# The first K load of a cached-attention decode kernel, issued as two halves with the half that is transposed first in front

## The chip, the cores and the metric

The kernel runs on one core of one Trainium2 chip. The metric is the device time of one execution in microseconds (us); lower is better. Every execution also has a span, from the first instruction to the last, which in these runs is 1.8 to 2.2 us shorter than the time.

## The reference, cut to what matters

One token attends to a cache of 65,536 positions with 8 key/value heads, two query heads to each. A small token MLP and a gate are mixed in at the end; they cost almost nothing (the page of the kernel before gives VectorE and ScalarE 0% each of the chain that ended last).

```python
# x: 1x1x448   k_cache, v_cache: 1 x 8 x 65536 x 256, bf16 (268 MB each)
q = (x @ wq).reshape(B, Sq, 16, 256).transpose(0, 2, 1, 3)
k = jnp.repeat(k_cache, 2, axis=1);  v = jnp.repeat(v_cache, 2, axis=1)
scores = jnp.einsum("bhqd,bhkd->bhqk", q, k) * (256 ** -0.5)
o = jnp.einsum("bhqk,bhkd->bhqd", softmax(scores), v)
a = o.transpose(0, 2, 1, 3).reshape(B, Sq, 4096) @ wo
return g * a + (1 - g) * b          # g: gate, b: token MLP
```

## The kernel before

The caches are streamed in 32 blocks of 8.39 MB for K and as many for V; I call them K0, V0, K1, V1 and so on. A block is 128 partitions of 128 rows (NV = 128), and HV = 64 is half of that. All large loads are issued by SyncE, in order, on one queue that spreads over 16 DMA engines (each load leaves 16 landing records in the trace, and by the page below q1 takes 99.5% of the time of 16 engines).

```python
for j in range(NP):                                   # SyncE, NP = 32
    last = j == NP - 1
    if j >= 1:
        eng.wait_ge(sem_tr[NB - 1], BODY * (j - 1) + DC)   # half of K(j-1) is transposed
    load(kring, A_k_cache, j, 0, HV if last else NV, HV * (j % 2), sem_k)
    if last:
        load(kring, A_k_cache, j, HV, NV, HV, sem_kb)
    if j == 0:
        eng.wait_ge(s_q, 1); eng.wait_ge(s_hb, 1)          # query projection is done
    else:
        eng.wait_ge(sem_pv, j)                             # values of block j-1 are done
    load(vbuf, A_v_cache, j, 0, NLATE if last else NV, 0, sem_v)
    # ... the pieces of the last V, and the output weights wo once per head
```

The K ring holds one and a half blocks. The V buffer holds one block. So V1 cannot be issued before the tensor engine (PE) has finished all the value matmuls of block 0, whatever the queue is doing.

On the PE a block is 8 chunks. Each chunk is transposed through PSUM, copied out by VectorE and ScalarE, and scored; then come the value matmuls of the whole block.

```python
def transposes(k, c, j, u16, x2):
    if k == 0:
        pe.wait_ge(sem_k, u16)            # u16 = 16 * (j + 1)
    if k == DC:                           # DC = 4
        with pe.If(j == NP - 1):
            pe.wait_ge(sem_kb, 16)
    # ... chunks 0 to 3 read rows 64 to 127 of an even block, chunks 4 to 7 rows 0 to 63

def values(j, c0, u16):
    # ... denominators, then 128 matmuls acc <- vbuf, pT
    some(0, NLATE).then_inc(s_early, 1)
    some(NLATE, NV).then_inc(sem_pv, 1)   # all but the last block
```

The softmax here doesn't subtract the row's maximum and nothing guards it: scores larger than these inputs give would overflow.

## Time and profile before

| | |
|---|---|
| time, median of 3 runs | 1267.47 us (1267.24 to 1267.68) |
| the profiled execution | 1268.64 us, span 1266.8 us |
| bytes read | 544.2 MB, 430 GB/s over the span |
| steady pace, from the landings | one block in 19.35 us, 433.5 GB/s |

These lines are from the page of the kernel before: the span, the bytes moved in 40 equal slices of it, and the queues with packets, MB and share of the 16 engines' time.

```profile
span 1266.8 us, 38663 instructions
...
GB/s 411 430 417 430 432 430 441 430 432 432 430 441 430 432 430 432 441 430 432 430 432 441 430 432 430 432 441 430 430 432 430 443 430 430 432 430 443 430 416 350
...
q1 hardware_dynamic: 12264, 544.22, 99.5%
q8 instruction: 8, 0.13, 0.0%
```

The q1 queue is the SyncE loads and fills the engines for 99.5% of the span: the kernel is bound by its loads.

The chain of waits of the kernel before, in its first 125 us, has the columns start, duration (both us) and what took it. "issue" is time in which the engine waited for nothing that the profile shows.

```profile
1.65 30.86 DMA kring<-in_A_k_cache_dram
...
32.64 6.43 PE kst L278 x32
...
49.55 0.85 issue
...
55.74 2.62 issue
...
60.99 2.01 PE acc L330 x28
63.00 2.77 issue
65.77 4.34 PE acc L330 x92
...
73.87 6.30 PE kst L278 x32
...
85.38 27.35 DMA kring<-in_A_k_cache_dram
```

The PE starts when K0 has landed, works through block 0 with stops of 0.85, 2.62 and 2.77 us that have no stated cause, and the chain follows the PE all the way into block 1 at 73.87 us.

The timeline of the SyncE queue (start us, duration us, engine, line, operation, tiles) shows when K1, V1, K2 and V2 were issued:

```profile
44.27 0.34 SPq L221 DMA_DIRECT2D kring<-in_A_k_cache_dram  x1
70.15 0.33 SPq L221 DMA_DIRECT2D vbuf<-in_A_v_cache_dram  x1
85.38 0.33 SPq L221 DMA_DIRECT2D kring<-in_A_k_cache_dram  x1
101.89 0.33 SPq L221 DMA_DIRECT2D vbuf<-in_A_v_cache_dram  x1
```

V1 goes out at 70.15 us. The stretches of one microsecond around it (start and end, length, busy time and instruction count of each engine, then PE clock, DMA share and GB/s) show the queue running dry:

```profile
69.00:70.00 1.00, 1.00 (x39) 0.68 (x31) 0.00 (x0) 0.00 (x0) 0.00 (x0) 1.00 0.91 393
70.00:71.00 1.00, 0.11 (x4) 0.00 (x0) 0.00 (x0) 0.00 (x0) 0.00 (x0) 1.00 0.07 16
71.00:72.00 1.00, 0.00 (x0) 0.00 (x0) 0.00 (x0) 0.00 (x0) 0.00 (x0) 1.00 2.17 786
72.00:73.00 1.00, 0.02 (x4) 0.03 (x4) 0.00 (x0) 0.00 (x0) 0.00 (x0) 0.70 0.67 262
```

A data packet is booked at its start and takes 2.42 us, so single microseconds swing widely. Read the 16 GB/s of 70 to 71 us together with the packets that were still in flight: counting those in the trace, the 16 engines lose 0.50 us each on average between 69.4 and 73 us, and under 0.05 us in all the rest from 5 to 1259 us.

### The profile page before, as it was taken

What the parts mean: (1) busy time and instruction counts of PE and PEld (TensorE: products, weight loads), DVE (VectorE), ACT (ScalarE), POOL (GpSimd) and SP (SyncE); (2) the same over time, 40 slices, a digit from 0 to 9 for tenths busy, and PEclk for the clock granted to TensorE, in tenths of its full rate; (3) what the DMA queues carried; (4) which work ended last, traced back from release to release, by engine and by line L of the source; (5) the groups of instructions that cost most, each with busy time, mean ns of one, the idle gap of its engine ahead of it and who ended that gap; (6) DMA issues with size and microseconds to landing.
All of it is one profiled execution on the core that took longest, in us unless ns stands there. A gap on an engine that the chain in (4) does not pass through costs nothing.

```text
span 1266.8 us, 38663 instructions
## 1 busy us (share of the span) xinstructions
PE 911.8 (72%) x17041; PEld 862.0 (68%) x17041; DVE 418.1 (33%) x741; ACT 537.4 (42%) x786; POOL 0.9 (0%) x7
## 2 busy tenths in 40 slices
PE   1886678766787666787666876768767688666698
PEld 1776668766677666686666876658766578665687
DVE  2433334333344233443222332223322233331233
ACT  0543345533355333454334553335533345432455
POOL 0000000000000000000000000000000000000000
PEclk9988789788898788888788888789887788887989
DMA  9999999999999999999999999999999999999998
GB/s 411 430 417 430 432 430 441 430 432 432 430 441 430 432 430 432 441 430 432 430 432 441 430 432 430 432 441 430 430 432 430 443 430 430 432 430 443 430 416 350
DMA packets 12365, 544.39 MB, mean 430 GB/s; under 512 B 1344, under 2 KB 3394, under 8 KB 3778
## 3 DMA queue, kind: packets, MB, share of 16 engines
q1 hardware_dynamic: 12264, 544.22, 99.5%
q8 instruction: 8, 0.13, 0.0%
q10 hardware_dynamic: 90, 0.01, 0.0%
q14 instruction: 3, 0.02, 0.0%
HBM read 544.22 MB, written 0.00 MB: 430 GB/s over the span
## 4 chain that ended last, share of the span: by engine, by line
DMA 68%; PE 30%; issue 1%; SPq 0%; DVE 0%; ACT 0%; ACTq 0%
DMA kring<-in_A_k_cache_dram 66%; PE kst L278 25%; PE sps L298 5%; DMA vbuf<-in_A_v_cache_dram 2%; PE acc L330 1%; PE sps L350 0%; SPq L221 0%; PE acc L322 0%; PE prj L370 0%; ACT pT L615 0%; SPq L218 0%; SPq L216 0%; DVE out_g L590 0%; PE prj L431 0%; DVE oTn L548 0%
## 5 line engine op out<-in xcount | busy, mean ns | idle before, releaser
L278 PE MATMUL kst<-ident,kring 128*128 128x128 f32 x4096 | 561.6, 298 | 310.5 <-DMA kring<-in_A_k_cache_dram 308.6
L626 ACT ACTIVATE ktT<-kst 128x1024 bf16<-128x1024 bf16 x512 | 499.6, 1021 | 668.1 <-PE kst L278 667.8
L278 PEld LDWEIGHTS kst<-ident,kring 128*128 128x128 f32 x4096 | 511.8, 155 | 320.2 <-issue 318.0
L532 DVE COPY ktT<-kst 128x1024 bf16<-128x1024 bf16 x512 | 354.3, 692 | 771.4 <-PE kst L278 748.1
L298 PEld LDWEIGHTS sps<-qcur,ktT 128*128 128x128 bf16 x8192 | 237.8, 96 | 6.5 <-issue 3.9
L298 PE MATMUL sps<-qcur,ktT 128*128 128x2 bf16 x8192 | 236.7, 163 | 3.5 <-issue 3.5
L330 PE MATMUL acc<-vbuf,pT 128*2 128x256 bf16 x4064 | 144.2, 310 | 3.5 <-issue 2.8
L330 PEld LDWEIGHTS acc<-vbuf,pT 128*2 128x2 bf16 x4064 | 107.4, 95 | 31.9 <-issue 3.3
L615 ACT ACTIVATE pT<-sps 128x32 f32 x256 | 51.8, 202 | 18.6 <-PE sps L298 18.6
L322 PE MATMUL acc<-pT,ones_sq 128*128 128x32 bf16 x256 | 11.7, 178 | 12.3 <-ACT pT L615 12.3
L322 PEld LDWEIGHTS acc<-pT,ones_sq 128*128 128x128 bf16 x256 | 8.6, 97 | 15.2 <-ACT pT L615 14.9
L632 ACT ACTIVATE z_b<-z_b 128x448 bf16<-128x448 bf16 x14 | 8.1, 577 | 20.5 <-DVE z_b L519 20.5
L537 DVE COPY accs<-acc 128x288 f32<-128x288 f32 x8 | 3.7, 458 | 39.6 <-PE acc L330 39.6
L394 PE MATMUL acc<-vbuf 42*128 42x42 bf16 x1 | 0.2, 216 | 8.6 <-DMA b_b<-in_B_b_dram 8.6
L523 DVE TENSOR_SCALAR z_b<-z_b 128x448 bf16<-128x448 bf16 x14 | 3.9, 277 | 6.8 <-ACT z_b L632 6.8
L394 PEld LDWEIGHTS acc<-vbuf 42*128 42x128 bf16 x1 | 0.1, 100 | 8.7 <-DMA b_b<-in_B_b_dram 8.7
L525 DVE TENSOR_TENSOR gu<-wtmp,z_b 128x448 bf16<-128x448 bf16 x14 | 5.5, 393 | 1.0
L517 DVE TENSOR_TENSOR z_b<-u_b,wtmp 128x448 bf16<-128x448 bf16 x14 | 5.5, 393 | 1.0
L513 DVE TENSOR_TENSOR z_b<-wtmp,u_b 128x448 bf16<-128x448 bf16 x14 | 5.5, 393 | 1.0
L511 DVE TENSOR_TENSOR wtmp<-u_b 128x448 bf16<-128x448 bf16 x14 | 5.5, 392 | 1.1
L507 DVE TENSOR_SCALAR wtmp<-hbT,params 128x448 bf16<-128x448 bf16 x14 | 4.7, 337 | 2.6 <-issue 2.6
L509 DVE TENSOR_SCALAR u_b<-wtmp,params 128x448 bf16<-128x448 bf16 x14 | 4.7, 336 | 2.6 <-issue 2.6
(84 smaller groups left out, 76.5 us busy)
## 6 DMA issues: line engine op xcount, KB each, us to landing
kring<-in_A_k_cache_dram SPq DMA_DIRECT2D x2, 4096.0 KB, 22.7
vbuf<-in_A_v_cache_dram SPq DMA_DIRECT2D x1, 6144.0 KB, 24.3
wo_sb<-in_A_wo_dram SPq DMA_DIRECT2D x8, 448.0 KB, 28.6
vbuf<-in_A_wq_dram SPq DMA_DIRECT2D x1, 3072.0 KB, 10.3
vbuf<-in_A_v_cache_dram SPq DMA_DIRECT2D x1, 1024.0 KB, 26.4
vbuf<-in_A_v_cache_dram SPq DMA_DIRECT2D x1, 768.0 KB, 27.4
vbuf<-in_A_wq_dram SPq DMA_DIRECT2D x1, 512.0 KB, 11.1
kring<-in_A_k_cache_dram SPq DMA_DIRECT2D x31, 27.9
```

The source lines that it names most:

```text
L278: ins = pe.transpose(kst[:, b, i * P:(i + 1) * P], kring_f[:, at + NT * (k % DC) + 4 * b + i, :], ident[:, :])
L298: ins = pe.matmul(sps[:, par, 2 * nt:2 * nt + 2], ktT[:, par, b, ntl * DH + dj:(ntl + 1) * DH:2], qcur[:, dj, :], start=(dj == 0), stop=(d ...
L322: pe.matmul(acc[:, DENC:SELC], ones_sq[:, :], pT[:, r, :], start=False, stop=(r == BODY - 1), skip_group_check=True)
L330: ins = pe.matmul(acc[o:o + REP, 0:DH], pT[:, r, 2 * nt:2 * nt + 2], vbuf[:, n, :], start=False, stop=False, skip_group_check=True)
L511: vec.tensor_tensor(W, U, U, op=ALU.mult)
L513: vec.tensor_tensor(Z, W, U, op=ALU.mult)
L517: vec.tensor_tensor(Z, U, W, op=ALU.add)
L525: vec.tensor_tensor(gu[:, :], W, Z, op=ALU.mult).then_inc(s_pb, 1)
L532: vec.tensor_copy(ktT[:, k % KTB, b, :], kst_b[:, b, :]).then_inc(sem_ev[b], 1)
L615: act.activation(pT[:, bass.ds(p0 + k % DC, 1), :].rearrange("p o n -> p (o n)"), sps[:, k % 2, 0:2 * NT], AF.Exp, scale=scale).then_inc(s ...
L626: act.activation(ktT[:, k % KTB, b, :], kst_b[:, b, :], AF.Copy).then_inc(sem_ev[b], 1)
L632: act.activation(z_b[:, :], z_b[:, :], AF.Tanh).then_inc(s_tanh, 1)
```

## The change

The intent is to let the PE start about 10 us earlier, as soon as the half of K0 that it transposes first has landed.

```diff
-                load(kring, A_k_cache, j, 0, HV if last else NV, HV * (j % 2), sem_k)
-                if last:
+                if j == 0:
+                    load(kring, A_k_cache, j, HV, NV, 0, sem_k)
+                    load(kring, A_k_cache, j, 0, HV, 0, sem_kb)
+                elif last:
+                    load(kring, A_k_cache, j, 0, HV, HV, sem_k)
                     load(kring, A_k_cache, j, HV, NV, HV, sem_kb)
+                else:
+                    load(kring, A_k_cache, j, 0, NV, HV * (j % 2), sem_k)
...
                 if k == DC:
+                    pe.wait_ge(sem_kb, 16)
                     with pe.If(j == NP - 1):
-                        pe.wait_ge(sem_kb, 16)
+                        pe.wait_ge(sem_kb, 32)
```

## The prediction

> **What bounds the kernel now.** The load queue. On the page the 16 DMA engines show nine tenths or more in 39 of 40 slices and the one SyncE queue takes 99.5% of their time; 544.2 MB move at 430 GB/s over a span of 1266.8 us. The landing records of the trace give the steady pace: one 8.39 MB K or V block lands every 19.35 us (K2 to V2, both last of 16 engines), that is 433.5 GB/s. [...] 544.2 MB at 433.5 GB/s are 1255 us. So only some 11 us of the span can be gained at all: about 1.7 us of start, the output projection's weights (small packets, 1.2 us per load against 1.06 at full pace), 1.3 us of staggered end pieces, about 4 us after the last landing, and one hole.
>
> **The hole.** In the timeline K0 lands at 32.5 us and the PE begins there. Its 8 chunks end at 60.2 us, of which 0.85 + 2.62 us are "issue" stalls; the value matmuls (with another 2.77 us of issue) end at 70.1 us, and only then is V1 issued (70.15). But K1, the last load in the queue, lands between 70.9 and 72.8 us, by engine. Counting the packets in flight, the engines are never idle between 5 and 70 us and between 73 and 1261 us, and lose 0.50 us each on average at 70 to 73 us. The engine that lands last loses more: K1 to V1 takes 72.8 to 93.4 = 20.6 us where the steady step is 19.35. So the hole costs about 1.2 us at the end. Every later V is issued about 11 us before the queue runs dry (V2 at 101.9, K2 landing 112.8).
>
> **What the change does.** The first half (64 of 128 rows) lands about 9.7 us earlier, near 22.8 us (estimate: 32.5 less half of 19.35). The query projection is done at about 17.5 us, so the PE starts then. Chunks 0 to 3 took 32.6 to about 44.5 us; they would end at about 35, when the second half (about 32.6 us) is already there. All chunks end at about 50. The values then wait for V0, which still lands at about 52.3, and end at about 58 to 62 us. V1 is issued near 60 instead of 70.15, ahead of K1's end at about 72.9, and the hole closes. K1's issue moves from 44.3 to about 34.5: no effect, V0 is still being moved.
>
> **Added.** Halved packets: 32 KB take 1.218 us, 64 KB 2.423 (trace); 16 of the one for 8 of the other per engine is +0.1 us. One more DMA issue, 0.43 us on an idle queue. One more satisfied semaphore wait per block on the PE, far from its limit.
>
> **Sum.** -1.2 + 0.1 = -1.1 us, out of 10 us by which the PE starts earlier: the other 9 turn into waiting for V0 and later loads. Predicted 1266.4 us, range 1264.8 to 1268.0. Faster by over 2%: 0.3%; within 2%: 99.2%; slower: 0.5%.
>
> **What would show it.** First transpose at 22 to 24 us. A new PE wait of about 2 us for V0 near 50 us. V1 issued at 58 to 63 us. K1 to V1 landings 19.35 us apart; all landings from V1 on about 1.1 us earlier; K0, V0, K1 landings unchanged within 0.3 us. Tail after the last landing unchanged, about 4 us.
>
> **What would make it wrong.** Issue stalls that grow so that V1 is still late (no gain); idle of the last engine that was not the hole but other traffic (gain near 0); difference between chips, larger than 1 us.

## More of the kernel before

Ahead of its loop the PE computes the query projection with 128 small matmuls written out one after another, which matters later.

The queue q8, which the profile labels "instruction", moved 8 packets.

## The result, and the profile after

| | median | lowest to highest | runs |
|---|---|---|---|
| before | 1267.49 us | 1267.24 to 1269.57 | 6 |
| after | 1267.45 us | 1267.26 to 1267.66 | 6 |

The ratio is 0.9997 with a 95% interval of 0.9984 to 1.0010: the same time. The medians differ by 0.04 us, and yet the spans of the two profiled executions differ by 1.1 us, as predicted. That disagreement is what the experiments were for.

The page after, the same lines:

```profile
span 1265.7 us, 38663 instructions
...
GB/s 412 428 429 437 431 435 433 433 431 437 431 433 435 431 433 437 429 435 435 431 433 433 433 435 435 431 427 439 433 435 435 425 433 439 433 435 429 431 426 353
...
q1 hardware_dynamic: 12408, 544.22, 99.6%
q8 instruction: 8, 0.13, 0.0%
```

The chain of waits after, in the first 130 us:

```profile
1.65 21.20 DMA kring<-in_A_k_cache_dram
22.85 5.80 issue
28.65 6.19 PE kst L284 x32
...
40.04 32.93 DMA kring<-in_A_k_cache_dram
...
73.10 6.15 PE kst L284 x32
...
84.45 27.22 DMA kring<-in_A_k_cache_dram
```

The first half of K0 lands at 22.85 us, but the first transpose comes 5.80 us of "issue" later, at 28.65. From there on the chain no longer runs through the value matmuls into block 1; it steps from the transposes of block 0 to the load of K1 and to block 1 when K1 has landed. The SyncE timeline and the stretches after:

```profile
40.04 0.34 SPq L221 DMA_DIRECT2D kring<-in_A_k_cache_dram  x1
64.12 0.33 SPq L221 DMA_DIRECT2D vbuf<-in_A_v_cache_dram  x1
84.45 0.33 SPq L221 DMA_DIRECT2D kring<-in_A_k_cache_dram  x1
100.97 0.33 SPq L221 DMA_DIRECT2D vbuf<-in_A_v_cache_dram  x1
```

```profile
69.00:70.00 1.00, 0.00 (x0) 0.00 (x0) 0.00 (x0) 0.00 (x0) 0.00 (x0) 0.50 0.91 393
70.00:71.00 1.00, 0.00 (x0) 0.00 (x0) 0.00 (x0) 0.00 (x0) 0.00 (x0) 0.50 1.13 475
71.00:72.00 1.00, 0.00 (x0) 0.00 (x0) 0.00 (x0) 0.00 (x0) 0.00 (x0) 0.50 0.94 393
72.00:73.00 1.00, 0.00 (x0) 0.00 (x0) 0.00 (x0) 0.00 (x0) 0.00 (x0) 0.50 1.06 459
```

V1 goes out at 64.12 us in place of 70.15, and no microsecond is empty: between 5 and 1259 us the engines lose under 0.05 us each. The landing records of the trace give the time at which the last of the 16 engines had delivered each block; they read, in us:

| last engine lands | K0 | V0 | K1 | V1 | K1 to V1 | last piece of V31 |
|---|---|---|---|---|---|---|
| before | 32.51 | 52.25 | 72.80 | 93.38 | 20.58 | 1263.09 |
| after | 22.85 and 32.66 | 52.26 | 72.97 | 92.33 | 19.35 | 1262.00 |

Up to K1 nothing has moved by more than 0.2 us. The hole is closed, and every landing from V1 to the end comes 1.05 to 1.1 us earlier than in that one execution of the kernel before.

### The profile page after: what moved, and what is told of

Same layout as the page of the kernel before. It is cut to its first block, busy times and chain, and to the rows that moved or that the text cites. A ratio compares the mean times of both kernels' runs of the same rounds, so it can differ in the third digit from the quotient of the medians.

```text
span 1265.7 us, 38663 instructions
## 1 busy us (share of the span) xinstructions
PE 911.9 (72%) x17040; PEld 861.1 (68%) x17041; DVE 418.2 (33%) x741; ACT 537.2 (42%) x786; POOL 0.9 (0%) x7
## 3 DMA queue, kind: packets, MB, share of 16 engines
q1 hardware_dynamic: 12408, 544.22, 99.6%
## 4 chain that ended last, share of the span: by engine, by line
DMA 70%; PE 29%; issue 1%; SPq 0%; DVE 0%; ACT 0%; ACTq 0%
DMA kring<-in_A_k_cache_dram 68%; PE kst L284 24%; PE sps L304 4%; DMA vbuf<-in_A_v_cache_dram 2%; PE acc L336 0%; PE sps L356 0%; SPq L221 0%; PE prj L376 0%; SPq L218 0%; SPq L216 0%; PE acc L328 0%; DVE out_g L596 0%; ACT pT L621 0%; DVE oTn L554 0%; ACTq L621 0%
```

## The experiments

Theory A: the hole at 70 us is open in only some executions of the kernel before; the profiled one was such an execution and the median one was not. Its rival, theory B: the hole is in every execution, and the change gives its gain back elsewhere. Theory C: the PE's late start at 28.65 us, and the stops called "issue", are waits for the PE's own instructions. Its rival, theory D: something of the half load itself holds the PE.

### 1. The kernel before again (b_again)

No edit.

> The kernel before, unedited. Theory A (the hole at 70 to 73 us is in only some executions of the kernel before): most runs have a span near 1265.6 us and a time near 1267.4, a few are 1 to 2 us longer, and a profile of a short run shows V1 issued early enough that K1 to V1 is 19.4 us. Theory B (the hole is in every execution and the change gives its gain back elsewhere when no profile is taken): all runs have a span near 1266.8 us, as the first profile had.

Five runs: 1267.33, 1267.20, 1267.39, 1268.66 and 1267.37 us, with spans of 1265.5, 1265.4, 1265.6, 1266.9 and 1265.6. The profiled execution was a short one. Its SyncE timeline:

```profile
65.20 0.33 SPq L221 DMA_DIRECT2D vbuf<-in_A_v_cache_dram  x1
83.98 0.33 SPq L221 DMA_DIRECT2D kring<-in_A_k_cache_dram  x1
```

The unchanged kernel issued V1 at 65.20 us here, K1 to V1 was 19.34 us, and no engine idled. The waits of the PE between 15 and 75 us (engine and line, what released it, total us, times, longest us) show why. First the "issue" waits of this execution, then those of the first profile of the same kernel:

```profile
PE acc L330 <- issue: 3.5, 1, 3.5
PE prj L431 <- issue: 3.0, 1, 3.0
```

```profile
PE sps L298 <- issue: 3.5, 2, 2.6
PE prj L431 <- issue: 2.9, 1, 2.9
PE acc L330 <- issue: 2.8, 1, 2.8
```

(A further "issue" wait of 0.6 us, at the loop's return in the long execution, comes after V1's issue and is left out.) The stops on the scores (L298, 3.5 us in two) are absent in the short execution. Between the two issues of V1 lie 4.95 us: 3.8 of them arise at these two stops, 0.9 in the first 32 transposes (6.43 us against 5.52), which no wait explains, and 0.2 in the values. Theory A holds for this pair of traces: the same program has the hole or not, by how long the PE takes over block 0, and most of the difference is those stops.

### 2. The changed kernel again (a_again, a_more)

No edit, on two chips.

> The changed kernel, unedited. Both theories: 1267.4 us, span 1265.6 to 1265.8, no run over 1268.2 under theory A, because V1 is issued some 9 us before the queue runs dry and no stall of a few us can open the hole again.

> The changed kernel, unedited, once more on whichever chip this is, for the spread. If theory A holds, all runs lie between 1267.2 and 1267.9 us while some of the runs of the kernel before beside it lie above 1268; the medians differ by under 0.4 us.

a_again: median 1267.49 us (1267.26 to 1267.54), V1 at 63.49 us. a_more: median 1267.56 us (1267.37 to 1267.69), V1 at 63.88 us. In both the engines never idle and K1 to V1 is 19.35 and 19.34 us. The 9 runs of the kernel before beside a_again had a median of 1267.80 (1267.41 to 1269.06), those beside a_more 1267.54 (1267.13 to 1269.47). Taking the result, a_again with b_again, and a_more together, 7 of 29 runs of the kernel before were over 1268 us and none of 16 of the changed one (highest 1267.69). The medians are 1267.53 and 1267.48, the means 1267.81 and 1267.48. (Nine more runs of the kernel before, on a third chip with no unedited changed runs beside them, had one over 1268.) If the tail is really gone, it was worth 0.33 us on average, far below 2%; the intervals of every set of rounds include 1. With 16 runs the missing tail is likely, not proved, from times alone.

### 3. The halves in the other order (swapped)

```diff
                 if j == 0:
-                    load(kring, A_k_cache, j, HV, NV, 0, sem_k)
                     load(kring, A_k_cache, j, 0, HV, 0, sem_kb)
+                    load(kring, A_k_cache, j, HV, NV, 0, sem_k)
```

> The first K load in two halves, but the half that is transposed first comes second, so the PE starts at 32.6 us as in the kernel before and only the packet size and the extra issue stay. Theory A: 1267.5 us (0.1 us for the smaller packets), with the rare longer runs of the kernel before. Theory B with the give-back in the halved packets: over 1268.4 us, the hole and the give-back together.

Median 1267.62 us (1267.53 to 1268.22), ratio 0.9998 (0.9984 to 1.0011). The profiled execution, the 1268.22 one, had V1 at 69.85 us, 0.27 us of mean idling and K1 to V1 of 19.99 us; its span was 1266.4 us. Splitting without the order brings the hole back into play, and shows no cost of 1 us for the smaller packets. That tells against theory B's give-back in the halved packets.

### 4. Holding V1 back (b_hold8, a_hold8, a_hold24, b_hold24)

The idle POOL engine waits for the values of block 0, fills a scratch tile N times, and only then lets SyncE issue V1. Eight fills delay V1 by 2.65 us.

```diff
+                if j == 1:
+                    eng.wait_ge(s_hold, 1)
                 load(vbuf, A_v_cache, j, ...)
...
+            eng.wait_ge(sem_pv, 1)              # POOL
+            for _ in range(N):
+                eng.memset(idle[:, :], 0.0)
+                eng.drain()
+            eng.sem_inc(s_hold, 1)
```

> The kernel before, with V1's issue held back by 8 fills on the idle POOL engine after the values of block 0, some 2 to 3 us. Theory A: a typical run has less than 1 us to spare, so the span grows by 1.5 to 3 us in every run, to 1267.5 to 1268.5. Theory B: the hole is open already, so the span grows by the whole 2 to 3 us over 1266.8, to 1269 to 1270. If the queue had slack of over 3 us there: no growth.

> The changed kernel with V1's issue held back by the same 8 fills, 2.6 us in the kernel before. Theory A (a V1 that is issued before about 68.5 us costs nothing): V1 goes out at about 66.5 us, K1 to V1 stays 19.35 us, and every run stays at 1267.3 to 1267.7 us, where the kernel before with the same hold had a median of 1268.65. Theory B (the change has a give-back of its own elsewhere): the same growth as in the kernel before, over 1 us.

> The changed kernel with three times the hold, some 7.5 us: V1 at about 71.5 us, after the first engines have run dry (70.7). Theory A: the hole opens again; K1 to V1 is 2 to 3.5 us over the steady 19.35 and the time 1269.5 to 1271.0. If the queue were not what bounds this stretch: 1267.5 still.

> The kernel before with 24 fills (7.7 us in the changed kernel) ahead of V1: V1 at 73 to 78 us. With the knee that the nine traces so far show (no cost up to an issue at 68.4 us), K1 to V1 is 19.35 us plus V1's issue less about 68.5, so 4 to 9 us more, and the span grows over 1265.6 by the same amount, to 1270 to 1275. If part of the lost time were given back later (slack elsewhere in the queue), the span would grow by less than K1 to V1 does.

| | times of the runs, us | V1 issued in the profile | K1 to V1, last engine | span of the profile |
|---|---|---|---|---|
| b_hold8 | 1267.57, 1269.18, 1268.44, 1268.85 | 68.71 | 19.66 | 1265.8 |
| a_hold8 | 1267.44, 1267.34, 1267.43, 1267.82 | 66.49 | 19.36 | 1265.7 |
| a_hold24 | 1267.74, 1267.95, 1269.63, 1269.84 | 68.33 | 19.35 | 1265.6 |
| b_hold24 | 1273.61, 1270.74, 1274.66, 1272.74 | 76.10 | 25.29 | 1271.5 |

The same hold of eight fills moves three of four runs of the kernel before over 1268 us and none of the changed one: the change buys room of a few us at this one point. Theory B had foreseen the same growth in both. Two reservations: b_hold8 ran on another chip than a_hold8, one on which three of nine unedited runs of the kernel before were over 1268 as well (one of nine beside a_hold8), so the times alone are weak and the traces carry this. And the expectation of b_hold8, growth of 1.5 to 3 us in every run, was missed: against 1265.6 its spans grew by 0.2, 1.8, 1.0 and 1.4 us. One run of a_hold8 was 0.12 us over its range. The expectation for a_hold24 was half a miss: two of its four runs, the profiled one among them, still cost next to nothing, because the values had ended at 60.6 us there, some 3 us earlier than in the other traces of the changed kernel, and V1 still went out at 68.33. In b_hold24 the hole is wide open. Its SyncE timeline and its stretches of 2 us:

```profile
76.10 0.33 SPq L223 DMA_DIRECT2D vbuf<-in_A_v_cache_dram  x1
```

```profile
68.00:70.00 2.00, 0.31 (x11) 0.01 (x3) 0.00 (x0) 0.00 (x0) 1.03 (x6) 1.00 1.07 459
70.00:72.00 2.00, 0.22 (x4) 0.09 (x4) 0.00 (x0) 0.00 (x0) 1.30 (x7) 0.80 0.04 8
72.00:74.00 2.00, 1.21 (x6) 1.22 (x7) 0.00 (x0) 0.00 (x0) 1.30 (x7) 0.50 0.00 0
74.00:76.00 2.00, 2.00 (x11) 2.00 (x10) 1.05 (x2) 1.02 (x1) 1.27 (x7) 0.50 0.00 0
```

The engines idle 6.00 us each on average, K1 to V1 is 5.94 us over the steady 19.35, and the span is 5.9 us over the 1265.6 us of a run without the hole. (By the expectation's rule, V1's issue less about 68.5, it would have been 7.6.) What was lost at this point was not given back later: 5.94 us at V1, 5.9 us at the end. V1's first packet starts at 77.06 us, 0.96 us after the issue.

Ordered by V1's issue, the fourteen traces show a knee:

```
trace      V1 issued   mean idling 60-100 us   K1 to V1, last engine   span
a_third      57.15          0.00                   19.35               1265.6
a_again      63.49          0.00                   19.35               1265.7
a_more       63.88          0.00                   19.34               1265.8
after        64.12          0.00                   19.35               1265.7
b_again      65.20          0.00                   19.34               1265.5
a_hold8      66.49          0.00                   19.36               1265.7
a_twice      67.97          0.00                   20.66               1266.6
a_hold24     68.33          0.01                   19.35               1265.6
b_third      68.44          0.15                   19.39               1265.7
b_hold8      68.71          0.13                   19.66               1265.8
swapped      69.85          0.27                   19.99               1266.4
before       70.15          0.50                   20.58               1266.8
b_twice      70.33          0.57                   21.32               1267.5
b_hold24     76.10          6.00                   25.29               1271.5
```

A V1 issued by 68.3 us costs no idling; each microsecond after about 69 cost up to a microsecond (0.50 us of idling at 70.15, 6.00 at 76.10). A V1 at 57.15 us was worth no more than one at 68.33: both spans are 1265.6 us. The exception is a_twice, to which I come below.

### 5. A shorter program ahead of the PE's loop (a_third, b_third)

The query projection keeps 32 of its 128 matmuls, so 96 fewer stand ahead of the loop. The result is wrong (the comparison with the reference passed all the same: its tolerance does not see this).

```diff
-                    for kt in range(WF):
-                        pe.matmul(sps[:, 1, j:j + 1], wq_a[...], xcol[:, kt:kt + 1], start=(kt == 0), stop=False)
-                    ins = pe.matmul(sps[:, 1, j:j + 1], wq_b[...], xcol[:, WF + a:WF + a + 1], start=False, stop=True)
+                    for kt in range(1):
+                        ins = pe.matmul(sps[:, 1, j:j + 1], wq_a[...], xcol[:, kt:kt + 1], start=True, stop=True)
```

> A wrong result on purpose: in the changed kernel the query projection has 32 matmuls in place of 128, with the loads as they are, so that the PE's program is 96 matmuls shorter before its loop. Theory C (the PE starts at 28.6 and not at 22.9 us because its next 16 KB of instructions land at 26.9 us behind the data of K0, and needs 1.7 us more): most of 16 KB fewer have to come first, and the first transpose starts at 22.7 to 23.5 us. Theory D (something of the half load itself, such as its landing or the clock, holds the PE): the start stays at 27.5 to 28.7 us. The time stays at 1267.3 to 1267.7 under both, as the hole is closed already.

> The same shorter program (wrong result on purpose) in the kernel before. Theory C: the PE starts at 32.6 us as before, but the instruction packets of block 0 come earlier against its work, the stalls called issue shrink from 9 us of the bad execution, V1 goes out before 66 us in every execution, and no run is over 1268.0 us. Theory D: one run in four is over 1268.2, as in the kernel before.

a_third's chain of waits, then its one wait for V0, then V1 in its SyncE timeline:

```profile
1.65 21.44 DMA kring<-in_A_k_cache_dram
23.09 0.68 issue
23.77 5.54 PE kst L284 x32
...
34.51 38.47 DMA kring<-in_A_k_cache_dram
```

```profile
PE acc L336 <- DMA vbuf<-in_A_v_cache_dram: 1.9, 1, 1.9
```

```profile
57.15 0.33 SPq L221 DMA_DIRECT2D vbuf<-in_A_v_cache_dram  x1
```

The first transpose moves from 28.65 to 23.77 us. The load is the same; only the program is shorter. That fits theory C and contradicts theory D (the number itself missed its range by 0.27 us). The PE now shows what I had predicted for the change itself: a wait of 1.9 us for V0, and V1 issued before 60. The time is 1267.39 us (1267.33 to 1267.49): seven more microseconds of room are worth nothing.

b_third failed its expectation: median 1267.65 us (1267.44 to 1268.63), two of five runs over 1268.5, V1 at 68.44 us. A shorter program alone does not keep the kernel before clear of the hole. The packets suggest why: the third one came only at 47.33 us, 14.5 us after the PE had begun at 32.88, and in a_third it came at 37.74, 14.0 us after the start at 23.77. So their pace in block 0 seems to follow the PE's start; two traces do not prove it.

The packet records of q8 in the traces tie the stops to the instructions. That q8, labelled "instruction" by the profile, carries the PE's program I infer from its count: 8 packets, but 7 with the shorter PE program of this experiment and 9 with the longer one of the next. Each packet is 16,384 bytes. All times are us:

```
execution   an instruction packet ends      the PE goes on      gap
before            48.88                         50.40           1.52
before            56.71                         58.37           1.66
before            64.41                         65.77           1.36
before            71.28                         72.98           1.70
after             26.93                         28.65           1.72
after             44.04                         45.57           1.53
after             50.95                         52.62           1.67
after             57.43                         58.79           1.36
after             64.18                         65.86           1.68
a_third           22.00                         23.77           1.77
```

Every stop called "issue" in block 0 of the traces before and after, bar one of 0.6 us at the loop's return in the kernel before, ends 1.4 to 1.7 us after such a packet. In the kernel before, the packet that ended at 26.75 us had arrived while the PE was still waiting for K0; that is why the wait was hidden there.

### 6. A longer program ahead of the loop (a_twice, b_twice)

The whole query projection is computed twice over, with the right result: 128 more matmuls ahead of the loop.

```diff
+            for _ in range(2):
                 for dj in range(2):
                     for h in range(HQ):
```

> The changed kernel with its query projection computed twice over (right result), 128 more matmuls before the PE's loop, about one instruction packet of 16 KB more. The extra work itself takes 3 to 4 us, from 15.5 to about 19 us, so it alone does not reach the landing of the half at 22.9. Theory C (the PE's start waits for its instructions, which come 16 KB at a time and some 6 to 7 us apart behind the data): the first transpose moves from 27.6 to 28.7 to 33 to 36 us, as late as without the change or later, V1 goes out at 68 to 72 us and some runs are over 1268. Theory D: the start stays at 27.5 to 29 us.

> The same longer program in the kernel before. Theory C: the start is then set by the instructions here too, 33 to 36 us, about where the changed kernel with the same addition has it, so that the change is worth nothing at all; V1 at 70 to 73 us, K1 to V1 1 to 3 us over 19.35, most runs over 1268. Theory D: the start stays at 32.6 us.

The first transposes of the two, from the timelines of the PE, first a_twice, then b_twice:

```profile
32.33 5.62 PE L284 MATMUL kst<-ident,kring 128*128 128x128 f32 x32 [9.72 <-issue]
```

```profile
36.11 5.07 PE L278 MATMUL kst<-ident,kring 128*128 128x128 f32 x32 [12.38 <-issue]
```

The start moves to 32.33 us in the changed kernel (under the expected range by 0.67) and to 36.11 in the kernel before (over it by 0.11), both released by "issue" and not by the load. They were expected about equal and lie 3.8 us apart, and so do the packets: the third one ended at 30.59 us in a_twice and at 34.38 in b_twice, 1.74 and 1.73 us before the PE's start. That ties the start to the packet once more; why the packet came at different times was not tested. Nine instruction packets are loaded in place of eight. All eight runs are over 1268 us: medians 1269.02 and 1269.29. With a longer program the change is worth 0.3 us by the medians of four runs each, which is not clear of the spread.

a_twice is the exception in the list: V1 went out at 67.97 us and no engine idled, but one engine delivered V1 1.3 us after the next to last (93.30 against 91.99), and the span is 1 us longer. The ninth instruction packet ran from 74.39 to 75.48 us, 1.09 us of one engine, while V1 was being moved. The records do not name the engine, but on a busy engine each packet starts within some 10 ns of the end of the one before it, so V1's chains of eight packets can be followed. The instruction packet lies in the chain that ended last, and the data packet after it took 2.89 us in place of 2.42: together 1.57 us. That engine had begun V1 at 71.97 us, when two others began later (72.15 and 72.17) and ended earlier. So the packet made it the last.

## Why the prediction was right or wrong

The time lay in the range and the class was right: within 2%. Neither says much, because no change at all (the median before, 1267.47) lies in the range and the class as well: that the number held is owed to the width of the range. The bound was right too: the load queue at 19.35 us per block decides, and no work of the PE appears in the time as long as the loads go out in time (V1 at 57.15 us and at 68.33: span 1265.6 both times). That the queue could go no faster than the measured 433.5 GB/s was my assumption; no run here tested it.

The mechanism was right for the execution that I had in front of me: the hole closed, K1 to V1 fell from 20.58 to 19.35 us, landings from V1 on moved by 1.1 us, and the span by 1.1 us. The halved packets cost about 0.1 us at K1, as estimated: its last landing is at 72.87 us on average over the eight traces with halves and at 72.76 over the six without, though single traces of one form differ by up to 0.34.

The step that failed is the baseline: "Predicted 1266.4 us" subtracts 1.1 us from the median time, 1267.47, although the hole had been seen in a profiled execution of 1268.64. The 1.17 us between those two numbers were in view before the prediction and are about the hole itself. The median execution of the kernel before has no hole (b_again: V1 at 65.20 us, span 1265.5), so there was nothing to take from the median. What is left is the rare longer run.

A second step failed without harm: "The query projection is done at about 17.5 us, so the PE starts then." The half did land at 22.85 us, but the PE started at 28.65, because its instructions landed at 26.93 (a_third: a shorter program started at 23.77 with the same load). So the 10 us that the split buys became 4, the chunks ended at 54.4 and not at 50, V1 went out at 64.12 and not "near 60", just past the upper end of the stated 58 to 63, and the "new PE wait of about 2 us for V0" did not appear. I had seen the "issue" stops and put them down as fixed lengths; they are arrivals, which held work back only where nothing else did (the packet that ended at 26.93 us held the PE until 28.65 in the changed kernel; the one at 26.75 in the kernel before cost nothing, as K0 landed at 32.51).

A third term was right in size but on another engine than the prediction says. The chains of packets, followed as in experiment 6, show it in the kernel before. The engine that ended K1 last, at 72.31 us, went on with V1 at once and lost nothing. The one that delivered V1 last (93.38) began it only at 72.75, and its first packet took 3.42 us in place of 2.42; no instruction packet lies in its chain. The instruction packet of 76.65 to 77.58 us lies in the chain that came second last (93.02). So the 1.2 us of that execution are the hole's own, as idling and then a slow first packet; eleven of the 16 first packets of V1 took over 2.5 us there, which costs 0.41 us per engine on top of the 0.50 of idling, against one of 16 in the changed kernel. In swapped, as in a_twice, it is the chain with the instruction packet (76.49) that ended last.

It also stays open why the same program's instruction packets come at different times (45.37 and 50.88 us in b_again, 47.83 and 55.69 in the profile before). They travel beside 2.42 us data packets on full engines, which makes a variable wait plausible; no run here took that apart.

No version beat both kernels: the traces with the hole closed, a_twice aside, have spans of 1265.5 to 1265.8 us whether V1 is issued at 57 us or at 68.

## What to carry to other kernels

Compare the time of the profiled execution with the median before costing what the profile shows: a defect seen in a run 1.2 us longer than the median may be exactly that difference. In this kernel, bound by one load queue, an earlier start of the compute was worth only what it did to the issue time of the next load that would otherwise have missed the queue's end (V1 issued at 57.15 or at 68.33 us: span 1265.6); in one like it find that issue, measure its room, and expect nothing beyond it until a run shows more. And when a stop has no visible releaser, look at the instruction packets: here, at the first pass through a long program with the load queue at 99.6% of the DMA engines' time, the code was what the PE waited for, and the earlier load uncovered 5.80 us of that wait.

## What else the traces show

- At the first pass, in the changed kernel, the PE stood still for 5.80 us after its data had landed (22.85 to 28.65 us), and for another 1.6 to 1.8 us three times in block 0 and its end. The instruction packets (q8: 8 packets of 16,384 bytes) come while the data loads take 99.6% of the engines' time; they arrived 6.5 to 10 us apart in block 0, and the PE went on only 1.4 to 1.7 us after a packet's end. No run here tested whether the branches of the loop play a part.
- In b_hold24, on an idle queue, the first packet of an 8.39 MB load started 0.96 us after the start of the issue and 0.63 us after its end. That is not enough to plan by: of the fourteen traces, the latest issue without idling to speak of was at 68.33 us (a_hold24), some 2.5 us before the first engine's landing of K1 (70.86).
- The 16 engines of the one queue did not stay in step: in b_again the first engine delivered the last piece at 1259.86 us and the last at 1261.96, and a spread of about 2 us was there from K0 on (30.61 to 32.61; V1: 89.89 to 92.06). The end of the kernel waits for the last of them: the span ended 3.7 us after the last landing both before (1263.09 of 1266.8 us) and after (1262.00 of 1265.7).
